# A gated S4D block with a ReLU feed-forward on one core: pools that wait by tile, first loads and spectra moved beside the kernel stage, late modulation as rows in 32-column tiles

## The chip, the core and the metric

The kernel runs on one core of one Trainium2 chip. The metric is the device time of one execution in microseconds; the time before is the median of three runs, 1528.92 us (1525.8 to 1534.64). The core has five engines that matter here: TensorE (PE in the profile, its weight loads PEld), VectorE (DVE), ScalarE (ACT), GpSimd (POOL) and SyncE (SP). Each runs its own queue in order. Loads and stores are issued by SP or by GpSimd, and a transfer that must wait for something holds up what stands behind it on the issuing engine.

## The reference, cut to what is computed

The input `u` has 2048 tokens of D = 576 channels, the state size is N = 128, the inner width Dff = 4608, all in float32.

```python
sa, ca, ga, sb, cb, gb = split(silu(c) @ w_mod, 6)        # six vectors of 576
h = layernorm(x) * (1 + ca) + sa
K[d, l] = 2 Re sum_n C[d, n] dt[d] exp(A[d, n] dt[d] l)    # l = 0 .. 2047
y = irfft(rfft(h, 4096) * rfft(K, 4096), 4096)[:2048]      # causal convolution
x = x + ga * (y + h * D_skip)
h = layernorm(x) * (1 + cb) + sb
x = x + gb * (relu(h @ w1) @ w2)
```

## The kernel before, in words

**Kernel stage** (`KGen.first`). The rows K[d, l] are sums over N of products of two exponentials: 16 coarse steps (`W1`) times 32 fine ones (`W2`). Six groups of 96 channels are worked through; in each, ScalarE makes sines and exponentials, VectorE and GpSimd double them to full tables, and TensorE sums their products into `kps` for the first 512 taps. The tables go to DRAM (`W2d`, `Zd`, `W1d`), for later taps are made from them during the feed-forward part (`KGen.rest`: `kps` matmuls of L402, the loads of L361, the stores of L343). The rows go to `ke` and from there to DRAM as `kd`. Three of the six modulation vectors are also made in this stage (`mod`).

**Block 0 of the convolution.** The 2048 tokens are four blocks of 512. `conv(s)` does for block s, in two halves of channels (p = 0, 1): load the tokens `x` and the kernel rows `kt`; the first norm (`stats`, `norms`, `norm1`, giving `h`); transforms of `kt` and `h` by DFT matmuls with the tables `fcU`, `fcK` into `Z`, by TensorE and ScalarE; a butterfly on VectorE from `Z` to a spectrum `K` or `U`; products of spectra `Y`, with those of earlier blocks read back from DRAM (`Ud`, `Kd`, `Rd`); a butterfly back to `V`; inverse matmuls `ps_i` with `gc`; the skip and gate; the second norm with output `h2`; TensorE transposes `ps_t`; and scaling to `xf`, split into a rounded part and its rest, `xh`, `xl`, with `xs` for the last 64 channels. A transform has two forms. `transform` makes 8 matmuls and leaves both levels of the butterfly to VectorE (L644); `transform1` (L681, L683) sums two matmuls into each output, 16 in all, with negated tables `fcUn`, `fcKn`, `gcn`, which does the first level in TensorE. Block 0 uses `transform1` throughout.

**Late modulation** (`mod_late`). The other three vectors `sb`, `cb`, `gb` are made beside block 0's convolution: 30 products each with the weights as the stationary operand and one moving column (L551). Two buffers hold the weights, loaded on SP.

**Feed-forward.** 36 chunks of 128 inner columns for each of the 4 blocks. A chunk has 14 matmuls of w1 into `hps` (L968), a ReLU into `hh` (ScalarE) and its rest `hl` (VectorE, L974), and 14 matmuls of w2 into five accumulators `acc` (L993). In block 0 the rounded weights' rests are made and stored to DRAM (`L1d`, `L2d`); later blocks read them. Four times in each chunk `step()` takes pieces of other work from a generator and writes them between the matmuls: in block 0 the later kernel taps in two passes (`kg.rest`) and then the convolution of block 1, in block 1 that of block 2, and so on. How much it takes follows from `rate(b)` times the number of steps so far, at most 2.7 units of VectorE work and 2 matmul pieces a step. What is left when a block's chunks are done is written behind the last one.

**What sets the order.** A framework places each engine's instructions at build time, mostly in order of their writing where data and buffers allow it; instructions marked `keep_in_program_order` stay where they are written. Buffers come from pools. When a pool is closed and another takes its memory, the first use of the new pool waits until the whole old pool is free:

```python
self.sm = ctx.enter_context(tc.tile_pool(name="sm", bufs=1))
```

All pools of `main` are opened so, over those of the kernel stage (`kg_c`, `kg_t`, `kg_ps`). At the start of each `kg.rest` pass and of each later `conv` the pool of the step before is replaced in the same way.

Of the kernel before, what the change touches and what calls it, by code (L numbers as in the profile page):

```python
# [18 lines left out]
P = 128  # L19
# [20 lines left out]
class KGen:  # L40
# [13 lines left out]
    def open(self, ctx):  # L54
        tc = self.tc
        self.pc = ctx.enter_context(tc.tile_pool(name="kg_c", bufs=1))
        self.pt = ctx.enter_context(tc.tile_pool(name="kg_t", bufs=1))
        self.ps = ctx.enter_context(tc.tile_pool(name="kg_ps", bufs=1, space=PSUM))

    def bank(self, name):  # L60
        return self.ps.tile([P, 512], F32, tag="ph", bufs=3, name=name)

    def setup(self, I):
        nc, pc, k = self.nc, self.pc, self.k
        v, kept = nc.vector.tensor_tensor, self.tc.keep_in_program_order
        tmp = lambda n: self.pt.tile([G, NG, P], F32, tag="W2", bufs=5, name=n)
# [15 lines left out]
        self.dl = pc.tile([G, NS, G], F32R, name="dl")  # L82
        dtb = dtT.unsqueeze(2).broadcast_to([G, NG, P])
        th = self.pt.tile([G, NG, P], F32, tag="T1", bufs=2, name="th")
        z = self.zz = [pc.tile([G, 2, NG, P], F32R, name=f"z{n}") for n in "tr"]
# [119 lines left out]
    def start(self, g, s15, c15):  # L205

        v, p = self.nc.vector.tensor_tensor, self.pool
        W1 = self.W1[g] = self.pt.tile([P, 2, 16, 2, H], F32, tag="W1", bufs=2, name=f"W1_{g}")
# [3 lines left out]
        t = self.pt.tile([P, 2, 2, H], F32, tag="Tc", name="tc")  # L212
# [10 lines left out]
    def powers(self, g, e, f):  # L223
# [4 lines left out]
        zs = self.pt.tile([P, 2, 2, G], F32, tag="zs", bufs=2, name=f"zs_{g}")  # L228
# [51 lines left out]
    def first(self, setup, mod):  # L280
# [12 lines left out]
        def values(g):  # L293
            E, F = EF.pop(g)
            W2 = W2s[g] = [
                self.pt.tile([P, 2, 32, H], F32, tag="W2", bufs=5, name=f"W2_{2 * g + u}")
# [23 lines left out]
        for g in range(NG):  # L320
# [5 lines left out]
            if g % 3 == 0:  # L326
                ke = self.pt.tile([P, 16, 72], F32, tag="ke", bufs=1, name=f"ke_{g}")
# [7 lines left out]
            if g + 2 < NG:  # L335
                raw(g + 2, lambda: rows(g, ps))
            else:
                rows(g, ps)

# [7 lines left out]
    def rest(self, psum, hs, blocks):  # L347
# [5 lines left out]
        with ExitStack() as ctx:  # L353
            pt = ctx.enter_context(self.tc.tile_pool(name=f"kr{hs[0]}{blocks[0]}", bufs=1))
# [38 lines left out]
            def products(h, W1, W2):  # L393
                if h % 6 == 0:
                    ke[0] = pt.tile([P, na, 72], F32, tag="ke", bufs=1, name=f"ker_{h}")
                for half in range(2):
                    ps = psum.tile([P, 6, na], F32, tag="cps", name="kps")
# [48 lines left out]
class Body:  # L446
# [3 lines left out]
    def build(self):  # L450
        nc, tc, I = self.nc, self.tc, self.I
        with ExitStack() as ctx:
# [14 lines left out]
            with ExitStack() as c2:  # L467
                kg.open(c2)
                setup = kg.setup(I)
                kg.first(setup, self.mod(kg))  # L470
            self.main(ctx, kg)
# [16 lines left out]
    def mod(self, kg):  # L488

        nc, I, pt = self.nc, self.I, kg.pt  # L490
# [5 lines left out]
        names = ((2, "ga", "W1", 2), (1, "ca", "W1", 2), (0, "sa", "W2", 5))  # L496
        ws = {}
        for i, nm, tag, bufs in names:
            w = ws[nm] = pt.tile([P, 5, D], F32, tag=tag, bufs=bufs, name=f"wm_{nm}")
            self.mod_weights(w, slice(i * D, (i + 1) * D))  # L500
# [9 lines left out]
        for i, nm, _, _ in names:  # L510
# [15 lines left out]
    def mod_weights(self, w, col):  # L526
        v = self.I["w_mod"]
        self.nc.sync.dma_start(
            out=w[:, 0:4], in_=v[0:512, col].rearrange("(k p) c -> p k c", p=P)
        )  # L530
        self.nc.sync.dma_start(out=w[:64, 4], in_=v[512:576, col])
# [9 lines left out]
    def mod_late(self):  # L541

        for i, nm in ((3, "sb"), (4, "cb"), (5, "gb")):
            w = self.cv.tile([P, 5, D], F32, tag="wm", bufs=2, name=f"wm_{nm}")
            self.mod_weights(w, slice(i * D, (i + 1) * D))
            yield
            ps = self.cps.tile([P, 512], F32, tag="cps", name=f"mps_{nm}")[:, :5]
            for j, o, n in ((4, 0, 64), (4, 64, 64), *((j, 0, P) for j in range(4))):
                for k in range(5):
                    kp = P if k < 4 else 64  # L550
                    self.nc.tensor.matmul(  # L551
                        ps[o : o + n, j : j + 1],
                        w[:kp, k, j * P : j * P + n],
                        self.ct[:kp, k : k + 1],
                        start=(k == 0),
                        stop=(k == 4),
                    )
            self.nc.scalar.activation(
# [615 lines left out]
```

## Time and profile before

| | |
|---|---|
| runs | 1534.64, 1525.8, 1528.92 us |
| profiled execution: own time, span | 1520.44, 1518.7 us |
| mean granted TensorE clock | 0.916 of full |
| busy: PE, PEld | 1349.1, 1070.7 us |
| busy: DVE, ACT, POOL | 868.2, 506.1, 170.0 us |
| transfers | 346.81 MB, mean 228 GB/s |
| first `hps` matmul of block 0 | at 311.4 us |
| length of blocks 0, 1, 2, 3 | 378.8, 310.9, 267.1, 250.5 us |

All times of the trace are counted from the span's start. The profiled execution is 8.5 us shorter than the median of the runs. A block's length runs from its first `hps` matmul to that of the next block, the last one's to the end of the span. In the lists of waits and chains a row has a start, a duration, an engine, the output and input, and the line; "<-" with a name in brackets tells what ended the idle time before it.

### The profile page before, as it was taken

Reading aid. Unit: us, or ns where it says so; the run is one execution under the profiler, and the core shown is the slowest. Engines: PE = TensorE matmul, PEld = TensorE weight load, DVE = VectorE, ACT = ScalarE, POOL = GpSimd, SP = SyncE. Lnnn points to the kernel's source line nnn. Section 1 sums busy time; section 2 is a strip of 40 time slices with the busy share of each in tenths; the row PEclk is TensorE's granted clock in tenths of the full one; section 3 lists DMA queues with packets and bytes.
Section 4 is the critical chain, followed back from the end, with each engine's and each line's share of the span. In section 5 each row is a group of like instructions: output and inputs, shape, how many; then the busy total and the mean of one; then the engine's idle time right before and its main releaser. Section 6 shows DMA issues by size and latency. Waiting matters only on the chain.

```text
span 1518.7 us, 26519 instructions
## 1 busy us (share of the span) xinstructions
PE 1349.1 (89%) x10880; PEld 1070.7 (71%) x10880; DVE 868.2 (57%) x1303; ACT 506.1 (33%) x910; POOL 170.0 (11%) x274
## 2 busy tenths in 40 slices
PE   5867359779999998769899998999999999999997
PEld 4656348557787765557677776777788788888885
DVE  6667432879965678683884597615699711111111
ACT  6566212232222233134123422533332433233332
POOL 3364500010011010001101100000000000000000
PEclk9855557979999999889999999999999999999998
DMA  5445673257769676638976889576789566666662
GB/s 181 183 178 231 231 233 148 94 204 261 241 223 400 228 252 243 256 103 288 353 248 225 308 293 350 160 214 200 272 325 382 177 187 199 206 197 197 197 196 71
DMA packets 116537, 346.81 MB, mean 228 GB/s; under 512 B 19584, under 2 KB 19872, under 8 KB 105408
## 3 DMA queue, kind: packets, MB, share of 16 engines
q1 hardware_dynamic: 97824, 218.88, 43.5%
q0 software_dynamic: 18368, 125.65, 21.8%
q8 instruction: 85, 1.39, 0.4%
q10 hardware_dynamic: 224, 0.59, 0.1%
q14 instruction: 36, 0.29, 0.1%
HBM read 261.31 MB, written 83.76 MB: 227 GB/s over the span
## 4 chain that ended last, share of the span: by engine, by line
PE 52%; issue 18%; DVE 10%; DMA 8%; ACT 1%; POOL 1%; SPq 0%; POOLq 0%; DVEq 0%; ACTq 0%
PE acc L993 19%; PE hps L968 19%; PE kps L402 5%; PE ps_f L644 3%; PE ps_i L838 2%; DVE Y L817 2%; DVE T L815 2%; DMA w<-L2d 2%; DMA w<-L1d 1%; PE ps_f L681 1%; DMA kt<-kd 1%; DMA L1d<-w 1%; PE ps_f L683 1%; DMA R<-Rd 1%; DVE Y L811 1%
## 5 line engine op out<-in xcount | busy, mean ns | idle before, releaser
L993 PE MATMUL acc<-hh,w 128*128 128x512 f32 x1296 | 430.1, 405 | 12.2 <-DMA w<-L2d 8.6
L968 PE MATMUL hps<-xh,w 128*128 128x512 f32 x1152 | 393.3, 401 | 0.0
L993 PE MATMUL acc<-hl,w 128*128 128x512 f32 x720 | 284.1, 407 | 19.4 <-DVE hl L974 19.4
L993 PEld LDWEIGHTS acc<-hh,w 128*128 128x128 f32 x1296 | 246.6, 192 | 67.5 <-DMA w<-L2d 9.9
L974 DVE SCALAR_TENSOR_TENSOR hl<-hps,hh 128x512 fp32r<-128x512 f32 x144 | 99.1, 688 | 334.1 <-ACT hh L973 333.9
L968 PEld LDWEIGHTS hps<-xh,w 128*128 128x128 f32 x1152 | 218.4, 191 | 46.8
L968 PE MATMUL hps<-xl,w 128*128 128x512 f32 x576 | 234.3, 407 | 0.0
L973 ACT ACTIVATE hh<-hps 128x512 fp32r<-128x512 f32 x144 | 86.0, 597 | 350.8 <-PE hps L968 337.3
L951 ACT ACTIVATE w<-r 128x576 fp32r<-128x576 f32 x144 | 98.8, 686 | 279.4 <-issue 189.7
L993 PEld LDWEIGHTS acc<-hl,w 128*128 128x128 f32 x720 | 137.7, 193 | 50.1 <-DVE hl L974 20.8
L968 PEld LDWEIGHTS hps<-xl,w 128*128 128x128 f32 x576 | 109.8, 191 | 23.7
L942 ACT ACTIVATE w<-r 128x640 fp32r<-128x640 f32 x144 | 105.5, 733 | 24.9 <-DMA L1d<-w 23.2
L968 PE MATMUL hps<-xs,w 128*128 128x512 f32 x288 | 99.5, 416 | 12.4 <-ACT xf L895 4.4
L402 PEld LDWEIGHTS kps<-W1r,W2r 128*32 128x32 f32 x3456 | 68.7, 146 | 32.7 <-issue 20.6
L402 PE MATMUL kps<-W1r,W2r 128*32 128x48 f32 (+2 forms) x3456 | 78.8, 238 | 8.6 <-issue 5.8
L817 DVE TENSOR_TENSOR Y<-Y,T 128x1152 f32<-128x1152 f32 x64 | 84.4, 1352 | 0.0
L272 PE MATMUL kps<-W,W 128*32 128x16 f32 x2304 | 40.8, 218 | 39.6 <-issue 23.7
L968 PEld LDWEIGHTS hps<-xs,w 128*128 128x128 f32 x288 | 54.9, 193 | 26.4 <-ACT xf L895 4.8
L272 PEld LDWEIGHTS kps<-W,W 128*32 128x32 f32 x2304 | 38.4, 151 | 44.4 <-issue 24.9
L1090 POOL DMA_DIRECT2D out_dram<-x x16 | 8.7, 544 | 508.1 <-DVE x L1088 508.1
L645 ACT ACTIVATE Z<-ps_f 128x288 f32<-128x288 f32 x96 | 39.1, 407 | 61.4 <-PE ps_f L644 61.4
L838 PE MATMUL ps_i<-V,gc 128*128 128x288 f32 x144 | 46.7, 457 | 13.8 <-DVE x L843 7.0
(198 smaller groups left out, 1595.2 us busy)
## 6 DMA issues: line engine op xcount, KB each, us to landing
r<-in_w_dram SPq DMA_DIRECT2D x144, 320.0 KB, 3.6
r<-in_w_dram SPq DMA_DIRECT2D x144, 288.0 KB, 3.4
w<-L1d SPq DMA_DIRECT2D x108, 320.0 KB, 3.0
w<-L2d SPq DMA_DIRECT2D x108, 288.0 KB, 3.1
W2r<-W2d POOLq DMA_DIRECT2D x18, 1536.0 KB, 9.4
W2d<-W SPq DMA_DIRECT2D x12, 1536.0 KB, 7.5
Ua<-Ud POOLq DMA_DIRECT2D x15, 1152.0 KB, 10.0
W<-W1d POOLq DMA_DIRECT2D x18, 768.0 KB, 10.0
```

The costliest lines, as they stand in the source:

```text
L272: self.nc.tensor.matmul(ps[32 * dd : 32 * dd + 32, 12 * u + q, :], W2[:, r, :, ch], W1[:, u, :, r, ch], start=(r == 0), stop=(r == 1),)
L402: nc.tensor.matmul(ps[32 * dd : 32 * dd + 32, q, :], W2[:, r, :, ch], W1[:, :, r, ch], start=(r == 0), stop=(r == 1),)
L644: nc.tensor.matmul(o, fc[:, n2, c, :], src(n2), start=True, stop=True)
L645: nc.scalar.activation(Z[:, n2, c], ps[:, :PC], AF.Copy)
L817: v(y, y, T, op=op or ALU.add)
L838: nc.tensor.matmul(ps[:, :PC], a, b, start=(i == 0), stop=(i == len(ops) - 1))
L942: nc.scalar.activation(w[:, 0], r, AF.Copy)
L951: nc.scalar.activation(w[:, 0:D], r, AF.Copy)
L968: nc.tensor.matmul(ps, a, x, start=(i == 0), stop=(i == 13))
L973: nc.scalar.activation(hh, ps, AF.Relu)
L974: nc.vector.scalar_tensor_tensor(hl, ps, 0.0, hh, op0=ALU.max, op1=ALU.subtract)
L993: nc.tensor.matmul(acc[i], a, x, start=(f == 0 and j in (0, 3, 6, 9, 12)), stop=(f == NF - 1 and j in (2, 5, 8, 11, 13)),)
```

## The change

Pools of `main` and of `kg.rest` are opened with `reuse_waits="tile"`: a tile of a new pool waits only for the old tiles that overlap it. The kernel stage's pools are laid out anew (`kg_a`, `kg_c`, `kg_t`, `kg_w`, two of PSUM), and their tiles are spread over these. The last group's tail, `rows(NG - 1)`, is not run by `first` but handed to `main`, and written inside the first norm.

Tables, `x` of block 0 and both of its `kt` are loaded on SP and have buffers of their own. In block 0, the first norm is written out before the first transform and kept in program order. Three of its four forward transforms (`U` of both halves, `K` of half 0) and the inverse of half 1 become the 8-matmul form; the table `fcUn` is gone, and the other negated ones are loaded later. Inputs are transformed in the order 0, 2, 1, 3. In the tail of block 0, two of the four `h2` and two of the five `xf` move to VectorE.

Late modulation is turned around: a 32-column copy `cb` of the vector c is the stationary operand, the weights move (25 products a vector, into rows of four 32-row tiles), and the rows are transposed back to columns. It starts at piece 60 of block 0's convolution instead of at piece 0, with one weight buffer, loaded on GpSimd's queue.

`step()` is also limited by the VectorE units taken in the last three steps (`room`), and the rates fall.

```diff
     def open(self, ctx):
...
+        pool = lambda n, **kw: ctx.enter_context(self.tc.tile_pool(name=n, bufs=1, **kw))
+        self.pa, self.pc, self.pt, self.pw = (pool(f"kg_{x}") for x in "actw")
+        self.ps, self.ph = pool("kg_ps", space=PSUM), pool("kg_ph", space=PSUM)
...
-            pt = ctx.enter_context(self.tc.tile_pool(name=f"kr{hs[0]}{blocks[0]}", bufs=1))
+            pt = k.pool(ctx, f"kr{hs[0]}{blocks[0]}")
...
     def mod_late(self):
...
+        cb = self.cv.tile([P, 5, 32], F32, name="cb")
+        nc.vector.tensor_copy(cb, self.ct.unsqueeze(2).broadcast_to([P, 5, 32]))
         for i, nm in ((3, "sb"), (4, "cb"), (5, "gb")):
-            w = self.cv.tile([P, 5, D], F32, tag="wm", bufs=2, name=f"wm_{nm}")
-            self.mod_weights(w, slice(i * D, (i + 1) * D))
+            w = self.cv.tile([P, 5, D], F32, tag="wm", bufs=1, name=f"wm_{nm}")
+            self.mod_weights(w, slice(i * D, (i + 1) * D), nc.gpsimd)
             yield
...
-            for j, o, n in ((4, 0, 64), (4, 64, 64), *((j, 0, P) for j in range(4))):
+            parts = [(32 * j, 0, j * P, P) for j in range(4)] + [(0, P, 512, 64)]
+            for group in (parts[:4], parts[4:]):
                 for k in range(5):
                     kp = P if k < 4 else 64
...
+                    for r, o, c, n in group:
+                        nc.tensor.matmul(
+                            ps[r : r + 32, o : o + n], cb[:kp, k], w[:kp, k, c : c + n],
...
+            nc.tensor.transpose(ps[:, 0:P], row[:, 0:P], self.ident)
+            nc.tensor.transpose(ps[:, P : P + 32], row[0:32, P:], self.ident[:32, :32])
...
+    def pool(self, ctx, name, **kw):
+        return ctx.enter_context(
+            self.tc.tile_pool(name=name, bufs=1, reuse_waits="tile", **kw)
+        )
...
-            nc.gpsimd.dma_start(out=t, in_=self.I[n])
-        self.ff = ctx.enter_context(tc.tile_pool(name="ff", bufs=1))
-        self.xp = [ctx.enter_context(tc.tile_pool(name="xa", bufs=1))]
+            nc.sync.dma_start(out=t, in_=I[n])
+        self.x2p = [self.pool(ctx, "x2a")]
+        self.ff = self.pool(ctx, "ff")
+        self.xp = [self.pool(ctx, "xa")]
...
             for i, _ in enumerate(self.conv(0)):
-                if i % 6 == 0:
+                if i == 40:
+                    for t, a in zip((self.fcKn, self.gcn), I["neg"]):
+                        nc.gpsimd.dma_start(out=t, in_=a)
+                if i == 60:
+                    late = self.mod_late()
+                if i > 60 and i % 6 == 0:
                     next(late, None)
...
     def transform(self, src, fc, Z, kept=False):
...
-        for n2 in range(4):
+        for n2 in (0, 2, 1, 3):
...
         rs = self.norms(st, kept)
         yield 2.0
+        if kept:
+            self.last_rows()
...
-        nc.gpsimd.dma_start(
+        (nc.gpsimd if s else nc.sync).dma_start(
             out=x2, in_=self.I["x"][s * 512 : (s + 1) * 512, :]...
...
         def mm_U(p, Z):
-            if s == 0:
-                return self.transform1(src, self.fcU, self.fcUn, Z)
-            return self.transform(src, self.fcU, Z)
+            return self.transform(lambda n2: hv[:, n2, :, p], self.fcU, Z, s == 0)
...
-            if s == 0:
+            if s == 0 and p == 1:
                 return self.transform1(src, self.fcK, self.fcKn, Z)
...
-            yield from self.butterfly1(Y, V) if s == 0 else self.butterfly(Y, V, 1)
+            yield from self.butterfly1(Y, V) if s == 0 and p == 0 else self.butterfly(Y, V, 1)
...
-        yield from both(self.norm1(x2, h), mm_K(0, ZK))
+        if s == 0:
+            yield from self.norm1(x2, h, True)
+            yield from mm_K(0, ZK)
+        else:
+            yield from both(self.norm1(x2, h, False), mm_K(0, ZK))
...
+            if s == 0 and n2 % 2 == 0:
+                nc.vector.tensor_scalar(
+                    h2[n2][:, :D], x2[:, n2], rs[n2][:, 0:1], rs[n2][:, 3:4], ...
...
+            if s == 0 and kk in (0, 2):
+                nc.vector.tensor_scalar(xf, ps, cb, sb, op0=ALU.mult, op1=ALU.add)
...
-        kt = self.cv.tile([P, 16, 72], F32, tag="kt", bufs=1, name="kt")
+        kt = self.cv.tile([P, 16, 72], F32, tag="kt", bufs=1 if s else 2, name="kt")
-        self.nc.gpsimd.dma_start(
+        (self.nc.gpsimd if s else self.nc.sync).dma_start(
...
+            room = (9.0, 7.0, 7.0, 7.0)[g // NF] - sum(recent[-3:])
+            recent.append(0.0)
-            while done[0] < target and v < 2.7 and pe < 2:
+            while done[0] < target and v < min(room, 2.7) and pe < 2:
...
     def rate(self, b):
-        return (2.25, 2.0, 1.7, 0.5)[b]
+        return (2.12, 1.8, 1.4, 0.5)[b]
```

Three places show how instructions move. In these lists a row is a line, an operation, and output<-inputs, with xN for N like it in a row; a number behind a name tells one buffer's use from another's.

SP at the end of the kernel stage, before: `W1d`, `W2d`, `Zd` are the last groups' tables, `kd_1` the last kernel rows, `wm` late modulation weights, `r` the first feed-forward weights.

```order
L323 DMA W1d_86<-W_4_1867 128x1536
L302 DMA W2d_75<-W_10_2225 128x3072
L302 DMA W2d_76<-W_11_2226 128x3072
L306 DMA Zd_99<-zs_2267 512x1x48
L306 DMA Zd_100<-zs_2267 512x1x48
L323 DMA W1d_87<-W_5_2232 128x1536
L323 DMA W1d_88<-W_5_2232 128x1536
L343 DMA kd_1_58<-ke_1666 64x1152 x2
L528 DMA wm_sb<-in_w_mod_dram 128x4x576
```

The same place after; the three tables stand ahead of `W1d_85`.

```order
L323 DMA W1d_86<-W_4_1876 128x1536
L762 DMA x_0_2556<-in_x_dram 128x2304
L302 DMA W2d_75<-W_10_2234 128x3072
L302 DMA W2d_76<-W_11_2235 128x3072
L306 DMA Zd_99<-zs_2276 512x1x48
L306 DMA Zd_100<-zs_2276 512x1x48
L323 DMA W1d_87<-W_5_2241 128x1536
L323 DMA W1d_88<-W_5_2241 128x1536
L948 DMA kt<-kd_0_57 128x16x72
L344 DMA kd_1_58<-ke_1675 64x1152 x2
L948 DMA kt<-kd_1_58 128x16x72
L963 DMA r_3055<-in_w_dram 128x640
```

`x` has come ahead of the last `W2d` stores, the first `kt` behind the last `W1d` stores and ahead of the last `kd` store, the second `kt` behind it; the `wm` loads have left this queue.

TensorE behind the last kernel products, before: `mps` are the late modulation's products.

```order
L272 MATMUL kps_2319<-W_5_2232,W_11_2226 32x16 x96
L681 MATMUL ps_f<-kt,fcK 128x288
L683 MATMUL ps_f<-kt,fcK 128x288
L681 MATMUL ps_f<-kt,fcK 128x288
L683 MATMUL ps_f<-kt,fcKn 128x288
L551 MATMUL mps_sb<-ct,wm_sb 64x1 x10
L551 MATMUL mps_sb<-ct,wm_sb 128x1 x20
```

The same place after, and below it, after a line of dots, the later place where the modulation now stands.

```order
L272 MATMUL kps_2328<-W_5_2241,W_11_2235 32x16 x96
L665 MATMUL ps_f<-kt,fcK 128x288 x8
L665 MATMUL ps_f<-h_2560,fcU 128x288 x16
L704 MATMUL ps_f<-kt,fcK 128x288
...
L557 MATMUL mps_sb<-wm_sb,cb 32x128 x20
L557 MATMUL mps_sb<-wm_sb,cb 32x64 x5
L566 MATMUL mpt_sb<-ident,row_sb 128x128
L567 MATMUL mpt_sb<-ident,row_sb 128x32
L862 MATMUL ps_i<-V_0_2772,gc 128x288 x4
L557 MATMUL mps_cb<-wm_cb,cb 32x128 x20
```

The three first transforms have 8 matmuls each and nothing between them; `sb` stands ahead of the first inverse matmul and `cb` in the midst of these.

TensorE at the boundary of blocks 0 and 1, before: `ps_t` are the next block's transposes, `xh_2944` and `acc_0` belong to block 0's last chunk, `xs_6304` to block 1.

```order
L893 MATMUL ps_t<-ident,h_6367 128x128
L968 MATMUL hps<-xh_2944,w_6387 128x512 x2
L968 MATMUL hps<-xl_2945,w_6387 128x512
L968 MATMUL hps<-xh_2944,w_6387 128x512
L993 MATMUL acc_0_3139<-hh,w_6453 128x512 x2
...
L993 MATMUL acc_0_3143<-hl,w_6453 128x512
L968 MATMUL hps<-xs_6304,w_6478 128x512 x2
```

The same place after.

```order
L1030 MATMUL acc_0_3151<-hh,w_6431 128x512
L1030 MATMUL acc_0_3151<-hl,w_6431 128x512
L928 MATMUL ps_t<-ident,h_6483 128x128
L928 MATMUL ps_t<-ident,h_6480 128x128
L928 MATMUL ps_t<-ident,h_6481 128x128
L928 MATMUL ps_t<-ident,h_6482 128x128
L928 MATMUL ps_t<-ident,h_6483 128x128
...
L1005 MATMUL hps<-xs_6415,w_6381 128x512 x2
L1005 MATMUL hps<-xs_6415,w_6478 128x512
L1005 MATMUL hps<-xh_6413,w_6381 128x512
```

The last transposes of block 1 stood ahead of the rest of block 0's last chunk; now they stand directly ahead of the first `hps` matmuls of block 1, and two chunks' `hps` begin side by side.

163 lines of the change are left out of this document (85 added, 78 removed).

## The prediction

> **What bounds it now.** I read the stretches first, cut at the first `hps` matmul of each token block (columns: stretch, length, busy us and count by engine, granted clock, DMA share, GB/s).
>
> ```profile
> 163.00:185.00 22.00, 7.73 (x424) 7.21 (x424) 7.62 (x15) 0.72 (x2) 8.75 (x12) 0.58 0.81 298
> 185.00:207.00 22.00, 0.00 (x0) 0.00 (x0) 3.47 (x13) 0.79 (x2) 3.33 (x5) 0.50 0.87 288
> 207.00:311.40 104.40, 89.47 (x392) 71.41 (x392) 53.55 (x100) 29.11 (x65) 4.38 (x7) 0.78 0.32 118
> 311.40:690.20 378.80, 335.50 (x3415) 258.73 (x3416) 291.38 (x388) 100.74 (x189) 33.11 (x60) 0.93 0.69 247
> 690.20:1001.10 310.90, 296.31 (x2301) 231.92 (x2300) 204.55 (x261) 100.10 (x183) 26.93 (x47) 0.97 0.78 274
> 1001.10:1268.20 267.10, 263.03 (x1149) 211.10 (x1148) 162.94 (x229) 95.98 (x171) 12.34 (x22) 0.99 0.73 250
> 1268.20:1518.70 250.50, 240.41 (x1071) 197.64 (x1069) 32.13 (x52) 73.70 (x116) 4.34 (x8) 0.98 0.59 180
> ```
>
> For 22 us after 185 no matmul runs; the 104 us that follow, the first convolution, end before any feed-forward matmul. The chain that ended last says what these stretches wait for:
>
> ```profile
> 184.77 0.50 ACT ke L49
> 185.82 2.76 DMA kd<-ke
> 191.47 15.34 DMA kt<-kd
> 207.38 1.30 PE ps_f L681 x2
> 208.68 0.96 PE ps_f L683 x2
> 211.56 9.18 PE mps_sb L551 x60
> 226.06 9.87 PE mps_cb L551 x60
> 241.72 7.77 PE mps_gb L551 x52
> 252.64 0.48 PE ps_f L681 x2
> 288.72 8.40 PE ps_i L838 x24
> 311.44 0.80 PE hps L968
> ...
> 1178.74 3.17 PE hps L968 x14
> 1181.92 3.17 PE acc L993 x14
> ```
>
> Three things carry 185 to 311: the kernel rows written to DRAM and read back (2.76 + 15.34 us), three modulation products of 27 us in which TensorE does nothing else, and transforms of two products each. The timeline gives VectorE's steps between them (start, length, engine, line, operation, and the idle time before it with its releaser; SPq is the issue of transfers on SP):
>
> ```profile
> 154.86 2.29 SPq L323 DMA_DIRECT2D W1d<-W  x2
> 169.78 0.95 DVE L261 TENSOR_TENSOR T<-W,Zp 128x768 f32<-128x768 f32 x1
> 203.28 2.98 DVE L690 BATCH_NORM_STATS2 st<-x 128x6 f32<-128x288 f32 x8 [32.55 <-DMA x<-in_x_dram]
> 206.17 0.41 DVE L699 BATCH_NORM_AGGREGATE mv<-st 128x2 f32<-128x12 f32 x4
> 206.47 1.28 ACT L700 ACT_TABLE_LOAD   x1 [21.21 <-DVE mv L699]
> 207.76 0.85 ACT L700 ACTIVATE mv<-mv,eps 128x1 f32<-128x1 f32 x4
> 212.32 1.54 DVE L725 SCALAR_TENSOR_TENSOR h<-h,mv,m_sa 128x576 f32<-128x576 f32 x2
> 289.83 0.75 DVE L657 TENSOR_TENSOR V<-Y 128x576 f32<-128x576 f32 x1
> 307.05 0.69 DVE L903 TENSOR_TENSOR xs<-xf,xs 64x512 fp32r<-64x512 f32 x1 [5.00 <-ACT xs L900]
> ```
>
> VectorE ends the kernel stage at 170.7 and then waits 32.6 us for x, which was queued behind the store of the kernel rows. In the feed-forward blocks 36 chunks of 3.17 + 3.17 us make 228 us of TensorE at least; the block lengths exceed it by 150, 83, 39 and 22 us (the last with the final output).
>
> **The change, part by part.** *Loads moved.* x, the DFT tables and both `kt` go to SP; x stands there ahead of the last two `W2d` stores, and its statistics between the last doublings. It is issued behind the `W1d` stores of the row at 154.9, so about 157; its landing is bounded by 3 us (the kernel rows' store, a quarter its size) and 12.3 (issued 191 before, used at 203.3). I take 7, for two stores of 1.5 MB are the only others then: 164, just when VectorE reaches it, and the 32.6 us go. What is late next: norm1 by itself. Two statistics inside the doublings add 2 x 0.37 (2.98 / 8), so they end at 171.5; six more 2.2, aggregate 0.4, table and roots 2.1, reciprocals about 1, eight `h` operations at 0.77 (1.54 for two) 6.2: 183. SP now holds the first `kt` load behind the last `W1d` stores, which wait for GpSimd: issued about 175, and its landing is bounded by 3 us (the kernel-row store, half its size) and 15.3 us. I take 9, since x and tables (2.7 MB) leave this stretch: 184. TensorE's last kernel products end at 184.7 as before. The second `kt` load on SP waits for the last kernel rows to land (2.8 us), and the feed-forward weight loads stand behind it: issued at about 190, and first split at 218, so nobody waits for them.
>
> The Trainium skill, DMA: Bandwidth & Descriptors, section "Issuing engines are not separate DMA queues", says that transfers from all engines share the same 16 DMA engines, and a second issuer saves only issue time. The first stretch above, at 0.81 share, agrees that there is little room in it; if nothing were gained by the move, the sum would be 9 us more (a rival below).
>
> *First spectra.* The first kernel transform and both of h become 8 products each with a second butterfly on VectorE, where there were 16. It starts at 185; four products at 0.96 and four at 0.48 us, and the order 0, 2, 1, 3 of inputs lets VectorE begin after four: 190. From here VectorE is the chain. Its rows (busy us, mean ns):
>
> ```profile
> L811 DVE TENSOR_TENSOR Y<-K,U 128x1152 f32<-128x1152 f32 x4 | 5.3, 1350 | 0.0
> L667 DVE TENSOR_TENSOR K<-Z 128x288 f32<-128x288 f32 x2 | 0.9, 452 | 0.0
> L944 DVE TENSOR_TENSOR w<-r,w 128x640 fp32r<-128x640 f32 x2 | 1.6, 823 | 0.2 <-ACT w L942 0.2
> ```
>
> A full butterfly is six at 0.75 and four at 0.45: 6.3 us; a product of spectra six at 1.3: 7.9. So three spectra 18.9 and the skip term 0.5 (209), product 7.9, weight split 0.8, half butterfly 3.0, K's second half 3.3, an output add 0.5 (225), product 7.9, full butterfly 6.3, three adds 1.4, splits 2.6 (243). TensorE's 8 + 16 + 16 products lie beside it. The added butterflies, 4 x 3.1 us net, are on the path; what they replace is TensorE time that was on it.
>
> *Late modulation.* Each vector becomes 25 products into 32-column tiles, 50 records, and two transposes. A record costs between 0.018 us (the kernel products, 3.40 us for 190) and 0.107 us (0.24 scaled from 288 to 128 columns): 1 to 5 us instead of 8 to 10. I take 4, and nothing on the path, because VectorE's products cover it; without that cover it is 3 x 4. The four extra copies a vector on ScalarE are covered by its idle time (29 us busy of 104). But there is now one weight buffer, on GpSimd's queue behind the spectrum saves, and the `cb` and `gb` products stand in TensorE's order ahead of inverse transforms. Each of these loads waits on GpSimd for the product before it; behind it stand the next saves and the first loads of block 0, which VectorE needs at 263. Landing of such weights:
>
> ```profile
> wm_cb<-in_w_mod_dram SPq DMA_DIRECT2D x1, 1152.0 KB, 16.6
> wm_gb<-in_w_mod_dram SPq DMA_DIRECT2D x1, 1152.0 KB, 6.1
> ```
>
> `cb` can be issued at about 216 and is reached at 221, so VectorE waits for an output add by 0 to 11 us; `gb` likewise. I take 3 in all, nearer the 6.1, since then only saves are in flight: 246.
>
> *Tail.* From the last butterfly (290.6) to `hps` (311.4) 20.9 us; 8 inverse products fewer save 3.9, and the two `h2` and two `xf` moved to VectorE I count as nothing (they fall into its 5.0 us of idle before `xs`; without that some 2 us more). First `hps`: 246 + 17 = 263, **48 us earlier** (36 if both weights are late, 57 with no wait at all).
>
> *Pools that wait by tile.* Loads of a new pool no longer wait for all of the old one:
>
> ```profile
> 313.31 0.53 POOL L361 DMA_DIRECT2D W<-W1d  x1 [33.38 <-DVE xl L905]
> 443.47 3.17 POOL L343 DMA_DIRECT2D kd<-ker  x6 [37.12 <-ACT ker L412]
> 452.00 0.53 POOL L361 DMA_DIRECT2D W<-W1d  x1 [5.36 <-PE hps L968]
> 532.20 0.54 POOL L735 DMA_DIRECT2D x<-in_x_dram  x1 [3.69 <-DVE w L944]
> ```
>
> VectorE begins its first rotation at 320; with the load ahead of `hps` it can begin 7 us sooner, and 5.4 and 3.7 us at the two later switches: 16 us of VectorE start in block 0, its busiest block (291 of 379).
>
> *Pace.* The rates fall from 2.25, 2.0, 1.7 to 2.12, 1.8, 1.4 and a sum over four steps is capped. Convolution work in a block is unchanged; counted in the code's own units (300, 250, 190) it ended about 2, 4 and 7 chunks before the block's end, and now ends in the last one or two. That spreads VectorE's load, so `hl` waits less behind it. The nearest rows are the excesses less the side work TensorE must do anyway (with each engine's rows for these tiles alone):
>
> ```profile
> 311.40:690.20 378.80, 55.86 (x2304) 48.36 (x2304) 8.13 (x24) 0.93 0.69 247
> 311.40:690.20 378.80, 24.13 (x64) 10.08 (x64) 13.05 (x32) 0.93 0.69 247
> ```
>
> Kernel products 56, transforms 64 x 0.24 = 15, inverse and transposes some 12 (an estimate from the same pitch) leave 66 us in block 0, and in the same way about 25 in block 1 and 6 in block 2. From -10 (work pushed onto the block ends) to -60 of 97; I take **24**: the 16, and 8 of pace.
>
> Sum: 1520.4 (the profiled execution, span 1518.7 and 1.7 around it) - 48 - 24 = 1448. The median of the runs, 1528.9, stands 8.5 above that execution, so I say **1457** on its scale.
>
> **Rivals.**
> - *Blocks give nothing* (20%): the convolution's chain of loads and products sets blocks 0 and 1, whatever the pace. For it: VectorE 291 of 379 us. Only the 48 stay: 1481.
> - *Blocks give half of the 97* (13%): the handovers were what made VectorE late everywhere: 1529 - 48 - 49 = 1432.
> - *Weights late* (8%): `cb` and `gb` land as the 16.6 us row, TensorE stands before the inverse: +12 on mine, 1469.
> - *No room for the moved loads* (4%): the engines of DMA are at 0.81 in 163 to 185, so 2.7 MB (three tables of 0.5 MB, x of 1.15) at 298 GB/s push `W1d`, `kt` or x back by 9 us: 1466.
> - *Cold TensorE* (6%): it waits for VectorE between short bursts, and each burst runs at 0.96 instead of 0.48 a product. 16 more products and 20 transposes on the path: 16 x 0.48 + 20 x 0.12 = 10 us, 1467. The rows at 207 and 252 show both speeds. The Trainium skill, TensorE: Matmul & The Clock Gate, Part 1, states the rule: half clock after an idle window of about 3.4 us, until as long a busy one; the trace agrees (0.50 granted in 185 to 207).
> - *Slower* (4%): the convolution now ends with the block, so its tail stands bare before the next block: in the new order the transposes come directly ahead of the next `hps`. At 20.9 us at three boundaries 63 are lost and 48 gained: 1544. It decides from 16 us a boundary with no other block gain; against it, most of the last chunk's `acc` still runs beside it.
>
> My forecast has 45%, its own range 1442 to 1472. The range over all is 1425 to 1495: it takes in blocks giving half and nothing, both unknown landings, and leaves the slower case out. 0.5% is 7.6 us, about what this kernel's runs can tell from no change: faster 94%, within 2%, slower 4%.
>
> **What would show it.** Right: first `hps` at 255 to 270; no wait of VectorE for x over 3 us; `kt` landing before 187; each modulation product under 5 us; restart of loads right behind the `kd` stores; blocks 355 to 365, 300 to 310, 263 to 269. Wrong: TensorE waiting on `wm_cb` or `wm_gb`; `kt` landing after 192; `hps` of the next block waiting over 10 us on `xs`; or longer gaps of issue in the kernel products, now that more transfers run beside them.

## The result, and the profile after

The changed kernel takes 1458.34 us (median of four runs, 1456.77 to 1468.38), the kernel before 1527.36 us beside it: the ratio is 0.9558, interval 0.95 to 0.9615. The profiled execution took 1456.77 us, its span 1455.0, its mean granted clock 0.928. The same stretches as before, cut again at the first `hps` matmul of each block (columns as in the prediction's first table):

```profile
163.00:185.00 22.00, 8.85 (x510) 8.35 (x511) 19.83 (x51) 2.71 (x7) 10.91 (x15) 0.61 0.95 341
185.00:207.00 22.00, 16.99 (x90) 12.16 (x89) 11.63 (x22) 11.12 (x27) 2.41 (x4) 0.78 0.72 245
207.00:259.80 52.80, 38.43 (x257) 26.61 (x256) 45.02 (x82) 11.81 (x35) 8.02 (x14) 0.82 0.82 296
259.80:640.70 380.90, 338.06 (x3421) 259.09 (x3421) 291.40 (x388) 100.69 (x190) 30.01 (x54) 0.94 0.67 236
640.70:939.50 298.80, 290.97 (x2297) 229.65 (x2296) 206.23 (x264) 101.59 (x188) 27.05 (x47) 0.98 0.80 282
939.50:1205.10 265.60, 261.25 (x1150) 210.22 (x1149) 163.36 (x230) 95.89 (x172) 12.37 (x22) 1.00 0.75 252
1205.10:1455.00 249.90, 241.10 (x1071) 198.14 (x1069) 32.14 (x52) 73.71 (x116) 4.36 (x8) 0.98 0.61 180
```

The first `hps` comes at 259.8 instead of 311.4: 51.6 us. Block 0 is 2 us longer, block 1 is 12 us shorter, blocks 2 and 3 change by 1.5 and 0.6. The sum is the 63.7 us by which the span fell. In the stretch after 163, VectorE is busy for 19.8 of 22 us where it was for 7.6, and the one from 207 to `hps` is half as long as it was.

The chain of waits from the last kernel rows to the late modulation:

```profile
187.57 0.94 PE kps L272 x39
189.58 7.14 DMA kd<-ke
197.20 4.67 DMA r<-in_w_dram
203.03 4.15 PE ps_f L665 x10
215.70 2.17 PE mps_sb L557 x50
226.38 2.97 PE mps_cb L557 x50
229.63 11.00 DMA wm_gb<-in_w_mod_dram
240.77 3.07 PE mps_gb L557 x50
```

Three modulation products of 2.2 to 3.1 us have taken the place of three of 7.8 to 9.9. The longest load in the chain is now `wm_gb` with 11.0 us, where it was `kt` with 15.3. The timeline gives VectorE's steps, and TensorE's wait for that weight:

```profile
168.55 0.46 DVE L713 BATCH_NORM_STATS2 st<-x 128x6 f32<-128x288 f32 x1 [1.82 <-DMA x<-in_x_dram]
184.37 0.81 DVE L752 SCALAR_TENSOR_TENSOR h<-h,mv,m_sa 128x576 f32<-128x576 f32 x1
187.34 0.45 DVE L779 TENSOR_TENSOR kt<-kt,dsk 1x288 f32<-1x288 f32 x1 [2.15 <-DMA kt<-kd]
193.11 0.76 DVE L679 TENSOR_TENSOR W<-Z 128x576 f32<-128x576 f32 x1 [5.33 <-ACT Z L666]
242.91 0.46 DVE L693 TENSOR_TENSOR V<-W 128x288 f32<-128x288 f32 x1
240.77 3.06 PE L557 MATMUL mps_gb<-wm_gb,cb 128*32 128x128 f32 x50 [4.48 <-DMA wm_gb<-in_w_mod_dram]
```

The 32.6 us that VectorE waited for x are 1.8. TensorE's wait of 4.5 us for `wm_gb` ends at 240.8, and the products behind it end at 243.8, where VectorE's last butterfly ends too (243.4).

### The profile page after: what moved, and what is told of

Its sections match the earlier page's. It is cut to its first block, busy times and chain, and to the rows that moved or that the text cites. A ratio compares the mean times of both kernels' runs of the same rounds, so it can differ in the third digit from the quotient of the medians.

```text
span 1455.0 us, 26336 instructions
## 1 busy us (share of the span) xinstructions
PE 1311.7 (90%) x10792; PEld 1036.7 (71%) x10792; DVE 879.8 (60%) x1326; ACT 503.0 (35%) x915; POOL 169.4 (12%) x273
## 4 chain that ended last, share of the span: by engine, by line
PE 49%; issue 20%; DVE 17%; DMA 9%; ACT 3%; POOL 1%; SPq 0%; POOLq 0%; ACTq 0%; DVEq 0%
PE hps L1005 16%; PE acc L1030 16%; PE kps L403 4%; DVE Y L841 3%; DVE T L839 3%; PE kps L272 3%; PE ps_f L665 3%; PE ph L127 2%; PE ps_i L862 2%; DMA L1d<-w 2%; DMA w<-L2d 2%; DMA Ua<-Ud 1%; DMA Ud<-U 1%; DVE T L372 1%; DVE hl L1011 1%
## 5 line engine op out<-in xcount | busy, mean ns | idle before, releaser
L1030 PEld LDWEIGHTS acc<-hh,w 128*128 128x128 f32 x1296 | 245.6, 191 | 78.3 <-DVE w L991 13.2
L1011 DVE SCALAR_TENSOR_TENSOR hl<-hps,hh 128x512 fp32r<-128x512 f32 x144 | 99.3, 690 | 317.3 <-ACT hh L1010 317.2
L666 ACT ACTIVATE Z<-ps_f 128x288 f32<-128x288 f32 x120 | 48.6, 409 | 67.6 <-PE ps_f L665 66.9
```

Source lines behind the costliest of these rows:

```text
L666: ev = nc.scalar.activation(Z[:, n2, c], ps[:, :PC], AF.Copy)
L1011: nc.vector.scalar_tensor_tensor(hl, ps, 0.0, hh, op0=ALU.max, op1=ALU.subtract)
L1030: nc.tensor.matmul(acc[i], a, x, start=(f == 0 and j in (0, 3, 6, 9, 12)), stop=(f == NF - 1 and j in (2, 5, 8, 11, 13)),)
```

## The experiments

The kernel stage itself does not end at the same time in every profile: its last kernel product ends between 184.3 and 191.7 us. The start is therefore best read as the time from there to the first `hps`. One profile of each kernel, in us; median and ratio come from the runs, and each ratio is to the kernel before, run beside it on the same chip.

| kernel | last kernel product | first `hps` | between | block 0 | block 1 | block 2 | median | ratio, interval |
|---|---|---|---|---|---|---|---|---|
| before | 184.7 | 311.4 | 126.7 | 378.7 | 310.9 | 267.1 | 1527.36 | |
| changed | 188.5 | 259.8 | 71.3 | 380.8 | 298.8 | 265.6 | 1458.34 | 0.9558, 0.95–0.9615 |
| changed, again | 191.5 | 264.2 | 72.7 | 381.2 | 302.2 | 267.7 | 1462.43 | 0.9583, 0.9536–0.9629 |
| no_overlap | 187.4 | 282.8 | 95.4 | 381.8 | 299.8 | 269.8 | 1482.17 | 0.9697, 0.966–0.9733 |
| spec_old | 188.2 | 276.8 | 88.6 | 376.8 | 299.4 | 268.3 | 1472.94 | 0.9622, 0.9578–0.9666 |
| spec_old_wm | 188.7 | 263.7 | 75.0 | 381.4 | 300.1 | 265.8 | 1461.55 | 0.9597, 0.9559–0.9634 |
| mod_old | 184.3 | 283.6 | 99.3 | 381.6 | 298.7 | 266.5 | 1483.86 | 0.9706, 0.9674–0.9738 |
| mod_old_wm | 187.9 | 287.4 | 99.5 | 380.9 | 298.8 | 267.7 | 1494.2 | 0.9784, 0.9741–0.9827 |
| before_rows | 186.9 | 289.9 | 103.0 | 375.3 | 309.8 | 266.3 | 1493.17 | 0.979, 0.9749–0.9831 |
| wm2e | 185.9 | 257.2 | 71.3 | 379.2 | 300.1 | 267.4 | 1460.16 | 0.9589, 0.9543–0.9636 |
| pace_old | 187.1 | 260.4 | 73.3 | 383.3 | 311.1 | 265.6 | 1469.8 | 0.962, 0.9584–0.9657 |
| blk_whole | 191.7 | 260.8 | 69.1 | 388.1 | 302.9 | 264.3 | 1464.66 | 0.9618, 0.9579–0.9656 |
| ua_early | 190.9 | 260.7 | 69.8 | 371.9 | 299.7 | 270.0 | 1458.81 | 0.9573, 0.9531–0.9616 |
| combo | 191.7 | 265.9 | 74.2 | 373.3 | 298.8 | 269.3 | 1456.89 | 0.9543, 0.9502–0.9585 |

**The changed kernel again.** 

> The changed kernel itself once more, on the same chip as combo: first hps within 2 us of 259.8, blocks within 3 us of 380.8, 298.8 and 265.6; it tells how far two profiles of one kernel lie apart.

The start missed its 2 us by 2.4, because the kernel stage ended 3 us later, and block 1 missed its 3 us by 0.4; the time between agrees within 1.4, block 0 within 0.4, block 1 within 3.4, block 2 within 2.1. Smaller differences than these between two profiles are not read below.

**The early loads and norm.**

```diff
-        self.pa, self.pc, self.pt, self.pw = (pool(f"kg_{x}") for x in "actw")
-        self.ps, self.ph = pool("kg_ps", space=PSUM), pool("kg_ph", space=PSUM)
+        self.pa = self.pc = pool("kg_c")
+        self.pt = self.pw = pool("kg_t")
+        self.ps = self.ph = pool("kg_ps", space=PSUM)
...
-                last = kg.first(setup, self.mod(kg))
+                kg.first(setup, self.mod(kg))()
+                last = lambda: None
```

(and whole-pool waits for the pools of block 0's convolution.) 

> The changed kernel with the kernel stage's pools laid out and waited for as before, and its last rows written ahead of the first norm again, so that x is issued behind the last store of the kernel rows; everything else stays changed. Theory (the loads and the norm beside the kernel stage's end are the largest part of the earlier start): the first hps moves from 259.8 to 273-282 and the time rises by 13 to 22 us. Rival (VectorE's chain of spectra sets the start, K's spectrum can be done first, and x has slack): first hps at most 266, time up by at most 6 us.

The start is 24 us later by the time between, the total 23.8 us higher by the medians: the theory's side, a little more than it said. In the kernel before, x stood on GpSimd's queue behind the load of `fcUn`, whose buffer was free only when the kernel rows had landed; in this run it stands on SP behind the same landing. The first row is of the kernel before, the others are VectorE's waits in this run:

```profile
189.32 0.57 POOL L584 DMA_DIRECT2D fcUn<-in_neg_dram  x1 [16.32 <-DMA kd<-ke]
187.64 0.32 DVE L548 COPY cb<-ct 128x160 f32<-128x160 f32 x1 [11.55 <-PE kps L273]
194.27 0.45 DVE L783 TENSOR_TENSOR kt<-kt,dsk 1x288 f32<-1x288 f32 x1 [6.31 <-DMA kt<-kd]
207.68 2.98 DVE L717 BATCH_NORM_STATS2 st<-x 128x6 f32<-128x288 f32 x8 [12.96 <-DMA x<-in_x_dram]
```

Together VectorE stands for 30.8 us between its last doubling and x, where it stood for 32.6 before. This run takes back the layout, the whole-pool waits and the place of the last rows at once, so what each of the three is worth is not shown.

**The spectra in 8 products.** All of block 0's forward transforms with `transform1`, and the inverse of half 1:

```diff
-            return self.transform(lambda n2: hv[:, n2, :, p], self.fcU, Z, s == 0)
+            src = lambda n2: hv[:, n2, :, p]
+            if s == 0:
+                return self.transform1(src, self.fcU, self.fcUn, Z)
+            return self.transform(src, self.fcU, Z)
...
-            if s == 0 and p == 1:
+            if s == 0:
                 return self.transform1(src, self.fcK, self.fcKn, Z)
```

> The changed kernel with all four forward transforms of block 0 and the inverse of half 1 in the 16-product form again, the negated tables loaded on SP ahead of kt. Theory (the 24 added forward products stand on the path at 0.48 us or more, against 9 us of butterflies saved on VectorE): first hps 4 to 10 us later. Rival (work is only moved from one engine of the chain to the other): first hps within 3 us of 259.8, time the same.

(The run also loads the negated tables on SP ahead of `kt`, and does not keep the first transforms in program order.) 17 us, more than either side had said. The chain of this run does not go through the products but through a weight of the late modulation:

```profile
230.63 0.76 POOL wm_cb L531
232.43 12.54 DMA wm_cb<-in_w_mod_dram
245.01 2.00 PE mps_cb L557 x18
```

With one weight buffer, `wm_cb` is loaded only when TensorE is through with `sb`, whose products stand behind the forward transforms. To separate the two, the weights were given two buffers and an earlier start, first in the changed kernel, then with the old spectra:

```diff
-            w = self.cv.tile([P, 5, D], F32, tag="wm", bufs=1, name=f"wm_{nm}")
+            w = self.cv.tile([P, 5, D], F32, tag="wm", bufs=2, name=f"wm_{nm}")
...
-                if i == 60:
+                if i == 46:
...
-                if i > 60 and i % 6 == 0:
+                if i > 46 and i % 6 == 0:
```

> The changed kernel with two buffers for the late modulation's weights, and this work started 14 pieces earlier in block 0's convolution, so that sb, cb and gb stand beside the last forward transform and ahead of all inverse matmuls. Theory (TensorE's 4.5 us wait for wm_gb and the products behind it stand on the path to hps): first hps at 251 to 257, time 3 to 8 us lower. Rival (VectorE's last butterfly, which ends at 243.4, sets it anyway): first hps at 258 or later, time within 2 us.

> The 16-product transforms of spec_old together with the two early weight buffers of wm2e. spec_old started hps 17 us later, but its chain runs through the weight loads that wait for the products. Theory (the single buffer chains the weights' loads to TensorE's place in the order, and most of the 17 us came through it): first hps at most 264 and within 9 us of wm2e. Rival (the products themselves cost the 17 us): first hps at least 13 us later than in wm2e.

wm2e's start of 257.2 lies between the two sides, but its kernel stage ended 2.6 us earlier: the time between is the same 71.3, and the median of 1460.16 is no lower. That is the rival's side as far as the total goes. From VectorE's last butterfly to `hps` it is 13.2 us here and 13.7 in combo (below), against 15.0 to 18.1 in five profiles with one buffer, so the wait for `wm_gb` may cost some 2 us at the end, which this run lost again ahead of it, where VectorE waited 5.8 us for `kt`. With the old spectra the same edit brings 88.6 down to 75.0. So of the 17 us, 13.6 came through weights that were loaded late, one behind the other. The edit changes both the number of buffers and the start of the work, so their shares are not separated. The 3.7 us that remain are within the spread: kernels whose starts are alike lie 4 us apart, and combo, with the new spectra and the same early weights, has 74.2. A cost of the 16-product form itself is not shown.

**The late modulation's form.** 

> The changed kernel with the late modulation's products in the old form (weights stationary, one moving column), at the same places and with the same single buffer. Theory (TensorE's time and the load that waits for the product before it are on the path together): each product takes 7 to 10 us instead of 2 to 3, the gb weights land 10 us later, first hps 10 to 16 us later. Rival (VectorE's products of spectra cover it): first hps at most 3 us later.

> The old products (weights stationary, one moving column) in the changed kernel with the two early weight buffers of wm2e. mod_old started hps 24 us later. Theory (as with the spectra, most of that came through the load chained to the product before it): first hps at most 270, 13 us behind wm2e or less. Rival (30 us of products on TensorE are themselves on the path): first hps at 275 or later.

(Both put back the old loop of L551 of the kernel before; the second also has wm2e's edit.) 99.3 and 99.5 us between, 28 us more than the changed kernel, with the early weights or without. The first run starts `hps` 24 us later, where its theory had 10 to 16; in the second the theory of the chain falls, and the rival holds: the products' own time is on the path. The first run's chain:

```profile
212.31 9.74 PE mps_sb L552 x60
222.33 6.52 DMA wm_cb<-in_w_mod_dram
228.99 11.76 PE mps_cb L552 x60
242.89 11.91 DMA wm_gb<-in_w_mod_dram
254.85 10.84 PE mps_gb L552 x52
```

From the other side, the row form alone in the kernel before:

> The kernel before with the late modulation alone changed to rows in 32-column tiles, at its old places, with its two buffers and its loads on SP. Theory (the products stood bare on TensorE's path): each takes 2 to 3 us instead of 8 to 10, first hps 15 to 21 us earlier than 311.4, time 13 to 21 us lower. Rival (VectorE's waits for x and kt or the weights' landing take their place): first hps at most 8 us earlier.

21.5 us earlier (23.7 by the time between), just beyond the theory's 21. The time fell further than the 13 to 21 us expected: it is 32 us lower by the medians (1525.37 for the kernel before on the same chip) and 26 by the profiled executions, of which blocks 0, 1 and 2 together give 5. Its products:

```profile
212.64 2.88 PE mps_sb L556 x50
219.48 2.17 PE mps_cb L556 x50
225.68 2.17 PE mps_gb L556 x50
```

**The pace.**

```diff
-            while done[0] < target and v < min(room, 2.7) and pe < 2:
+            while done[0] < target and v < 2.7 and pe < 2:
...
-        return (2.12, 1.8, 1.4, 0.5)[b]
+        return (2.25, 2.0, 1.7, 0.5)[b]
```

> The changed kernel with the rates 2.25, 2.0, 1.7 and without the limit over four steps. Theory 1 (block 0 kept its length because the slower pace starts block 1's convolution later, which cancels the earlier pool handovers): block 0 falls from 381 to 360-368, block 1 goes back from 299 to 305-311, the time is 5 to 15 us lower. Theory 2 (block 0's length is set at its end, by the convolution's loads and saves beside the feed-forward loads, whatever the pace): block 0 375-385, block 1 305-311, the time 5 to 13 us higher.

The numbers are theory 2's: block 0 383.3, block 1 back at 311.1, the time 11.5 us higher by the medians. Its reason, what happens at the end of block 0, is not tested here but below. The slower pace is worth 12 us in block 1; the 2.5 us in block 0 lie within the spread of profiles. Rates and limit were undone together, so their shares are not known. Block 1 of this run (the same columns as above):

```profile
643.60:954.80 311.20, 294.92 (x2302) 231.33 (x2302) 204.25 (x261) 99.92 (x183) 26.94 (x47) 0.98 0.79 274
```

TensorE stands for 16.3 us (311.20 less 294.92) where it stands for 7.8 with the new pace, and is busy for 4 us more.

**The handovers.**

```diff
-            self.tc.tile_pool(name=name, bufs=1, reuse_waits="tile", **kw)
+            self.tc.tile_pool(name=name, bufs=1, **kw)
+            if name[:2] == "kr" or name in ("xb", "cv1", "cv2")
+            else self.tc.tile_pool(name=name, bufs=1, reuse_waits="tile", **kw)
```

> The changed kernel in which only the pools of the later kernel taps and of the convolutions of blocks 1 to 3 wait for the whole of the pool before, as before the change. Theory (in block 0 the pace decides when pieces are written between matmuls, so a handover that ends sooner is only slack): blocks 0 and 1 within 4 us of 381 and 299, the time within 5 us of 1458. Rival (the handovers were worth their 16 us, and something else took them): block 0 at 390 or more, time up by 10 us or more.

Between the two: block 0 is 388.1, 7 us longer, outside the 376.8 to 381.8 of all runs that share the changed kernel's pace, pools and loads in that block. GpSimd's waits at the three handovers are back at what they were before (33.4, 5.4 and 3.7 us):

```profile
265.78 0.57 POOL L362 DMA_DIRECT2D W<-W1d  x1 [32.44 <-DVE xl L944]
412.68 0.53 POOL L362 DMA_DIRECT2D W<-W1d  x1 [6.09 <-DVE w L994]
495.85 0.53 POOL L764 DMA_DIRECT2D x<-in_x_dram  x1 [3.62 <-DVE w L994]
```

Counted by chunks, 3.9 us of the 7 stand there by chunk 6, nothing is added at the second handover, and the rest comes behind chunk 23, after the third. So the handovers by tile are worth about 7 us in block 0, not 16. Block 1's 302.9 lies 0.7 above the changed kernel's second profile, which tells nothing.

**The end of block 0.** VectorE's longest wait for a load there in the changed kernel:

```profile
545.10 2.63 DVE L839 TENSOR_TENSOR T<-K,Ua 128x1152 f32<-128x1152 f32 x2 [6.01 <-DMA Ua<-Ud]
```

```diff
-        return self.cv.tile([P, 4, 2, PC], F32, tag="S", bufs=6, name=name)
+        return self.cv.tile([P, 4, 2, PC], F32, tag="S", bufs=7, name=name)
...
         Z1 = self.spec("Z")
+        if s:
+            pre[0] = self.load(self.Ud[0][0], "Ua")
```

(and `product` takes `pre[0]` for its first pair.) 

> The changed kernel with a seventh buffer for spectra, and the load of the first saved spectrum Ua of blocks 1 to 3 written ahead of the saves of K and U instead of behind them. Theory (the end of block 0 is set by VectorE standing 6.0 us before its products for Ua, with the weight splits of three chunks queued behind it): block 0 at 366 to 376, blocks 1 and 2 1 to 5 us shorter, time 6 to 18 us lower. Rival (VectorE's 291 us of work in a block and the transfers beside it set the end whenever Ua lands): block 0 at 378 to 384, time within 4 us.

```profile
529.84 1.35 DVE L841 TENSOR_TENSOR T<-K,Ua 128x1152 f32<-128x1152 f32 x1
260.70:632.60 371.90, 337.03 (x3420) 258.43 (x3421) 291.10 (x388) 101.04 (x190) 29.93 (x54) 0.95 0.69 245
```

The wait is gone and block 0 is 9 us shorter, 8 of them TensorE's idle time (34.9 instead of 42.8 us). The rest of the theory did not come: blocks 1 and 2 are no shorter (299.7 and 270.0), and the median of 1458.81 is not below the changed kernel's. A longer wait stayed, and nothing was tried on it: VectorE stands 10.5 us for a weight `w` of L981 at 595.4 in the changed kernel, and 11.1 us in this run. With wm2e's edit:

> The edits of wm2e (two weight buffers, late modulation 14 pieces earlier) and ua_early (a seventh spectrum buffer, Ua loaded ahead of the saves) together. If both hold apart from each other: first hps at 257, block 0 at 370 to 374, the time 6 to 12 us below after_again on the same chip. If what ua_early gave in block 0 is given back in later blocks, as its page's block 2 may say: within 4 us of after_again.

Block 0 is 373.3, as expected, but the first `hps` came at 265.9 and not at 257: the kernel stage ended at 191.7, and the time between is 74.2, no better than the changed kernel's. The median is 5.5 us below the changed kernel's on the same chip, but the intervals (0.9502 to 0.9585 and 0.9536 to 0.9629) overlap. That this version beats the changed kernel is not shown.

## Why the prediction was right, and where it was not

The time forecast was 1457 and the measured one 1458.34, and it was faster. That closeness is partly chance: three terms were off and their errors cancel. On the profiled scale the forecast was 1448 and the measurement is 1456.77. The start gained 51.6 instead of 48, the blocks 12 instead of 24, and the median stands 1.6 above the profiled execution, where I had carried over the 8.5 of before.

**The start was right step by step.** x was used at 168.6 (164 taken), `h` was complete at 185.2 (183), `kt` at 187.3 (184), the last kernel products ended at 188.5 (184.7), the first butterfly began at 193.1 (190), the last ended at 243.4 (246), and the tail took 16.4 us (17). The early steps are 2 to 5 us late, but most of that is the kernel stage itself: its fourth group ends at 141.7 instead of 139.1, ahead of the first moved load, which SP issues at 154.0. In mod_old, with the same early loads and a kernel stage that ran as before (its fourth group ends at 138.1), x was used at 164.3, `h` was complete at 180.9, `kt` at 182.5, and the last kernel products ended at 184.3, none more than 0.3 us behind the forecast. In 163 to 185 the DMA share is 0.95 at 341 GB/s where it was 0.81 at 298: the moved loads do fill a nearly full set of engines. The Trainium skill, DMA: Bandwidth & Descriptors, "Issuing engines are not separate DMA queues", says that transfers started by any engine run on the same 16 DMA engines, and the trace agrees in the share; the rival's price of 9 us did not come. Of the 3 us set down for late weights at most half came: VectorE's waits for output adds ahead of its last butterfly are 1.4 and 0.2 us. `wm_gb` took 11.0 us to land, and TensorE did wait for it, which the prediction had named as a sign against it; wm2e, with 0.8 us of this wait, has the same time between.

**Late modulation was right in size.** I counted 4 us a vector and put the products under VectorE's cover. They take 2.2 to 3.1 us. What the prediction did not say is its share: before_rows shows that this part alone is worth some 22 us of the start, about as much as the early loads (24). The parts overlap: taken back one at a time they cost 24, 17 and 28 us, more than the 51.6 (55 by the time between) they give together. The order of the inputs and the `h2` and `xf` moved to VectorE were not tried alone.

**The block term failed, at two of its steps.** The blocks gave 12 us instead of 24, all of it in blocks 1 to 3, and the signs "355 to 365" and "300 to 310" were missed by block 0's 380.8 and, on the good side, by block 1's 298.8. The first step is "leave 66 us in block 0" (67 by its own terms), and 25 in block 1. I took what the side work's estimated time left over as time that could be won. But TensorE's idle time stands in the quoted rows: 378.80 less 335.50 is 43.3 us in block 0 and 310.90 less 296.31 is 14.6 in block 1. The remainder lies inside TensorE's busy time, where a pace can win little: in block 1, between pace_old and the changed kernel, 8.4 of the 12.4 us are idle time and 4.0 are busy time. The second is "16 us of VectorE start in block 0". A pool that is free sooner moves a load, but the piece that uses it is written between matmuls at a place that the pace sets, so blk_whole finds 7 us, not 16. And those 7 do not show in block 0's length, for the second pass of later kernel taps became longer. Counted by chunks, pace_old is 0.7 us ahead of the kernel before at chunk 17, loses 7.5 us in chunks 17 to 22, wins 4.4 in chunks 23 to 27, and loses 2.3 in the rest. At the same pace, chunks 17 to 22, before and in pace_old:

```profile
461.10:532.80 71.70, 66.11 (x1322) 52.70 (x1321) 43.01 (x48) 14.77 (x30) 8.02 (x16) 0.95 0.80 303
409.30:488.50 79.20, 68.70 (x1322) 54.22 (x1321) 44.73 (x49) 15.27 (x31) 9.64 (x17) 0.89 0.77 280
```

The same 1322 matmul records take 7.5 us longer: 2.6 us of busy time, at a clock of 0.89 instead of 0.95, and 4.9 us of standing. The waits of the kernel products that the profile gives no releaser for are 8.7 instead of 4.9 us:

```profile
PE kps L402 <- issue: 4.9, 4, 2.4
PE kps L403 <- issue: 8.7, 4, 3.8
```

The prediction had named longer gaps of issue there as a sign against it. All twelve profiles of the changed kernel and its variants have 7.4 to 9.1 us of them in these chunks, with the old pace (8.7) and with whole-pool waits (7.6) too; before_rows has 0.5. The traces point at what TensorE waits for: from the first `hps` on, the fourteen profiles have 58 such "issue" waits of over 1 us, and 45 of them end 2.2 to 2.7 us after a packet of 16 KB starts on the queue that the profile calls "instruction". A profile has about 62 such packets in these 1200 us, so that chance alone would put some 3% of the waits there. In pace_old three of the waits in these chunks end at 433.0, 446.1 and 461.3, and such packets start at 430.7, 443.6 and 458.9. So TensorE most likely waits there for its own instructions to be loaded; no run tested it, and why it waits longer in the changed kernel is not settled.

**The pace** was set down at 8 us and gave 12, in block 1 rather than in block 0. Its mechanism, work spread so that TensorE stands less, is what pace_old shows for block 1.

Of the rivals, "blocks give nothing" is true of block 0 alone. "Slower", the tail bare at each boundary, did not come: the convolution's end moved into block 0's last two chunks, which take 36.5 us instead of 15.0, but block 0 as a whole kept its length. "Cold TensorE" came only as far as the prediction had counted it: the granted clock is 0.78 in 185 to 207, where it was 0.50 without products, and the first ten records of the first transform start 0.48 us apart, the later ones 0.24. A price beyond that does not show: VectorE's chain from its first to its last butterfly took 50.3 us, where 53 without late weights were forecast.

## What to carry to other kernels

Count what a stage can gain from its busy column: length less TensorE's busy time is most of what better pacing can win (8.4 of 12.4 us in block 1), and work that only looks like waiting stays. A resource freed earlier is worth time only where the order lets the next user come earlier too; where a pace or a list sets the place of the work, more than half of it can be slack (7 us of 16 here). A single buffer chains a load to the place of its last reader in another engine's order, and then a lengthening ahead of that reader can be paid a second time: old spectra cost 17 us with one weight buffer, and at most 4 with two and an earlier start. Before a stage is said to end late by a change, look where its lateness begins: here most of it stood ahead of the first moved load.

## What the runs showed of the hardware that was not expected

In mod_old, sixty records with one moving column took 9.7 and 11.8 us, 0.16 to 0.20 each; in the changed kernel, fifty with 64 or 128 moving columns took 2.2 to 3.1, 0.04 to 0.06 each. The trace shows two parts of this. With 128 stationary columns and one moving column, records start 0.11 us apart at the full granted clock and 0.21 apart at half of it. With 32 stationary columns, four records for the four 32-row tiles start within 0.03 us, and the next four some 0.11 us after the first at full clock: the four run side by side.

The granted clock fell to half in the midst of the one-column products of `sb`, and stayed there through those of `cb`, though the profile has TensorE busy all the time in both. These two stretches of mod_old (columns as above; the clock stands ahead of the last two):

```profile
212.30:222.10 9.80, 9.80 (x62) 9.62 (x61) 9.80 (x13) 0.44 (x2) 0.00 (x0) 0.64 0.33 110
229.00:240.80 11.80, 11.80 (x61) 11.62 (x61) 0.00 (x0) 0.03 (x1) 0.00 (x0) 0.50 0.01 1
```

The kernel stage ended 7 us apart between profiles of kernels in which nothing of it differs (184.3 in mod_old, 191.7 in combo), and 3 us apart in two profiles of the changed kernel itself, which is as much as several of the effects studied here.
